# Pooled attention and two MLPs on one core: flat keys and values, longer query reads, low words on VectorE

## The chip, the cores and the metric

One core of a Trainium2 chip runs the kernel. The metric is device time in microseconds, from the first to the last instruction of one launch with a little around it; lower is better. The engines are TensorE (PE: matrix products into PSUM), VectorE (DVE: elementwise work and reductions), ScalarE (ACT: elementwise functions with a scale and a bias), GpSimd (POOL: elementwise work in SBUF) and SyncE (SP: it issues DMA). GpSimd also issues some DMAs. Each engine runs its instructions in order; semaphores order them between engines.

## The reference

```python
# q, k, v: (8, 8, 576, 64); pool = 8, Sp = 576 / 8 = 72
k_p = k.reshape(B, H, Sp, pool, D).mean(axis=3)
v_p = v.reshape(B, H, Sp, pool, D).mean(axis=3)
scores = np.matmul(q, k_p.transpose(0, 1, 3, 2)) / np.sqrt(D)
attn = softmax(scores)                          # exp, sum + 1e-9, divide
x = np.matmul(attn, v_p)                        # -> (B*S, H*D) = (4608, 512)
h = x @ moe_w_in                                # (512, 2048)
x = np.where(h >= 1, h, np.where(h <= -1, 0, (h + 1) ** 2 / 4)) @ moe_w_out
h = x @ moe2_w_in
return (h * sigmoid(h)) @ moe2_w_out            # (4608, 512)
```

So there are 8 batches of 576 queries, each with 72 pooled keys and values per head, and two MLPs over all 4608 rows. The weights arrive as 64-bit floats, and the kernel reads them as pairs of 32-bit words.

## The kernel before

**Number form.** Each MLP product is made from two half-precision words, high and low: `three` adds high x high, high x low and low x high in one PSUM accumulation. Every weight is converted on the chip. For each piece of a weight the chain is: `look` (VectorE, the largest magnitude), a scale found from it by `w_scale` (six tiny VectorE instructions on as many columns as there are pieces in the group), `signed` (ScalarE, line 208), `shifted` and `with_low` (VectorE, lines 109 and 216), a scaling pass on ScalarE (283 or 240), a cast to the high word on ScalarE (285 or 245), and the low word as a subtraction (286 or 246). The constants LO1 and LO2 say which pieces of the first MLP's two weights have that subtraction on VectorE: pieces 3 and 7 of the first weight, piece 0 of the second. GpSimd makes the others. The first weight has nine pieces (seven of 256 columns and two of 128), the second eight.

**Attention.** Query rows go in 36 tiles of 128. Tiles 0 to 3 make up token tile 0, the 512 rows of the first product. For tiles 0 to 8 (batches 0 and 1) attention runs in 32-bit floats: `att_qT` transposes the queries on TensorE, `att_scores` multiplies with the pooled keys in block form (`k32`), finds the largest score per head and subtracts it on VectorE, and exponentiates on ScalarE; `att_norm` sums, takes the reciprocal on VectorE and multiplies on GpSimd; `att_T` transposes the weights head by head (eight transposes); `att_pv` multiplies with the pooled values (16 matmuls) and `split` writes the high and low words of x. Later tiles use half-precision words and DMA transposes.

Keys and values are pooled by sums. In batch 0 the keys come head by head, 72 partitions of 2 KB each, and are reduced on VectorE, two heads on GpSimd; the values come in two halves of four heads and are summed by GpSimd (`halving`). From batch 1 on half of each group of eight rows is loaded, the other half is added by an accumulating DMA that GpSimd issues (`kv_more`), and VectorE adds the rest (lines 468 and 471).

**Order.** The code is emitted in the order wanted, and the framework places instructions on the engines by its own estimate of time. `tick` releases the parts of the conversion at steps that lists name: LOOK_AT, SCALE_AT, C1_AT (the nine pieces of the first weight), B1_AT (keys and values of batch 1), W2_AT and MORE2_AT (the second weight), SLOTS_AT (attention of tiles 4 to 7). Steps below zero lie in the attention of tiles 0 to 3, steps 1 to 18 in the first product of token tile 0 (`emit_h`, one step per 128 columns of 2048; `pre_A`, `min_A`, `mid_A`, `post_A`, `split_g` then apply the activation), later steps in its second product (`yA`). Each released part is held behind the last product, activation and VectorE instruction before it (`behind`). SyncE issues the loads in order: keys of batch 0, queries, values, the nine pieces, the later queries, batch 1, the second weight. The first weight's last four pieces are loaded into the room of the second weight's tiles w2[0] to w2[3].

After token tile 0 the kernel runs the remaining eight token tiles of the first MLP and then the second MLP with TensorE full.

Of the kernel before, what the change touches and what calls it, by code (L numbers as in the profile page):

```python
# [11 lines left out]
I32 = mybir.dt.int32  # L12
# [22 lines left out]
def tile_pooled_attention_two_mlps(  # L35
# [99 lines left out]
    cols, free, free2 = const.tile([128, 136], F32, name="cols"), iter(range(46)), iter(range(45))  # L135
    spread = cols[:, 46:136].rearrange("p (n u) -> p n u", u=2)
# [4 lines left out]

    def apart(n):
        i = [next(free2) for _ in range(n)][0]
        return spread[:, i:i + n, 0]
# [47 lines left out]
    def w_scale(e, d, s, g, up=14):  # L192


        t = sm.tile([128, 8, 2], F32, tag="wt", name="wt", bufs=2)[:, :, 0]
        a, b = (t[:, 4 * i:4 * i + g.shape[1]] for i in range(2))
        ts(a, g, FLOOR_HIGH, DOWN, ALU.max, ALU.mult)
        ts(b.bitcast(I32), a.bitcast(I32), EXP_MASK, op0=ALU.bitwise_and)
        bits(d, b, -1.0, 15 + TOP)
        ts(b.bitcast(I32), a.bitcast(I32), 0x00700000, 3, ALU.bitwise_and, ALU.logical_shift_left)  # L200
        bits(s, b, -1.0, 254 - 8 * TOP + up)
        ts(e.bitcast(I32), a.bitcast(I32), 0x7FF00000, 3, ALU.bitwise_and, ALU.logical_shift_left)
# [11 lines left out]
    def with_low(x, r):  # L214
        xi = x.bitcast(I32)
        return nc.vector.scalar_tensor_tensor(  # L216
            out=xi, in0=low(r), scalar=29, in1=xi, op0=ALU.logical_shift_right, op1=ALU.bitwise_or
        )

    def steps(piece, dst, scale, loaded, fill=None):  # L220
# [17 lines left out]
        def s3():  # L238
            x = t["x"]
            nc.scalar.activation(out=x, in_=x, func=AF.Copy, scale=scale()[1])  # L240
            if fill:
                fill(x)
                return
            hi, lo, eng = dst()
            nc.scalar.copy(out=hi, in_=x)  # L245
            eng.tensor_tensor(out=lo, in0=x, in1=hi, op=ALU.subtract)  # L246
# [7 lines left out]
    def weight_in(w, e, tiles, cuts, rooms):  # L254
# [4 lines left out]
        mx, s, g, down = (apart(n) for _ in range(4))  # L259
# [16 lines left out]
        def work(p):  # L276
# [6 lines left out]
            nc.scalar.activation(out=x, in_=x, func=AF.Copy, scale=s[:, p:p + 1])  # L283
            hi, lo = tiles[p][:, 0], tiles[p][:, 1]
            nc.scalar.copy(out=hi, in_=x)  # L285
            (nc.vector if p in LO1 else nc.gpsimd).tensor_tensor(out=lo, in0=x, in1=hi, op=ALU.subtract)  # L286
# [99 lines left out]

    SPT = (SP + 15) // 16 * 16
    NE = 2 * S // 128
    v16 = [bp.tile([SP, 2, H, D], F16, name=f"v16{j}") for j in range(2)]
    v32 = [x.rearrange("p a h d -> p (a h d)").bitcast(F32).rearrange("p (h d) -> p h d", h=H) for x in v16]  # L390
    both16 = bp.tile([128, 2, 2, 4, 128], F16, name="e16")
    e16 = [both16[:, j] for j in range(2)]
    km, vm = col(), col()
# [23 lines left out]

    def kv_load(b, which):
        if (b, which) == (0, "k"):
            for h in range(H):  # L420
                r = gp.tile([128, 2, N], F16, tag="g", name="k0").rearrange("p a n -> p (a n)").bitcast(F32)
                r = kv_raw[b, which, h] = r[0:SP].rearrange("p (r d) -> p r d", r=POOL)
                nc.sync.dma_start(out=r, in_=k[0, h].rearrange("(p r) d -> p r d", r=POOL))
            return
        if b == 0:
            src = v[0].rearrange("h (p r) d -> p h r d", r=POOL)
            for j in range(2):
                r = kv_raw[b, which, j] = kvp.tile([SP, 4, POOL, D], F32, tag="raw", name="v0", bufs=2)
                for a, b_ in PARTS:
                    nc.sync.dma_start(out=r[a:b_], in_=src[a:b_, 4 * j:4 * j + 4])  # L430
            return
# [3 lines left out]

    def kv_more(b, which):
        for a, b_ in PARTS:
            nc.gpsimd.dma_start(
                out=kv_raw[b, which][a:b_], in_=kv_rows(b, which)[a:b_, :, HALF:POOL], accum_op=ALU.add
            )  # L440

    def halving(to, r):

        plus(r[:, 0:4], r[:, 0:4], r[:, 4:8])
        plus(r[:, 0:2], r[:, 0:2], r[:, 2:4])
        plus(to, r[:, 0], r[:, 1])

    def kv_pool(b, which, j):
        if j == 0 and which == "v" and b < 2:
            sums[b, which] = v32[b]  # L450
        elif j == 0:
# [3 lines left out]
        if (b, which) == (0, "k"):  # L455
            for h in (2 * j, 2 * j + 1):
                r, to = kv_raw.pop((b, which, h)), sums[b, which][0:SP, h]
                if h in K_POOL:
                    halving(to, r)
                else:  # L460
                    nc.vector.tensor_reduce(out=to, in_=r.rearrange("p r d -> p d r"), axis=AX.X, op=ALU.add)
        elif b == 0:
            if j < 2:
                r = kv_raw.pop((b, which, j)).rearrange("p h r d -> p r h d")
                halving(sums[b, which][0:SP, 4 * j:4 * j + 4], r)
        elif j == 2:
# [25 lines left out]
    def keys32(b):  # L492
        ps = att_ps([128, NP, 128])
        x = sums.pop((b, "k"))
        for p in range(NP):
            nc.tensor.transpose(
                out=ps[:, p, 0:SP], in_=x[0:SP, 2 * p:2 * p + 2].rearrange("p h d -> p (h d)"),
                identity=ident[0:SP, 0:SP],
            )
        for h in range(2):  # L500
            r = slice(64 * h, 64 * h + 64)
            nc.scalar.copy(out=k32[b][r, :, h], in_=ps[r, :, 0:SP])
# [16 lines left out]
    def values_mean(b):  # L519
        junk = v16[b % 2] if b > 1 else ap.tile([SPT, H, 2, D], F16, tag="krows", name="by", bufs=2)[0:SP]  # L520
        sums_mean(sums[b, "v"][0:SP], vm, junk)

    def values_scale(b):
        if b not in vscale:
            vscale[b] = search(SP, vm, ev[:, b:b + 1])
# [17 lines left out]
    def load_q(i):  # L543
        if i == NI - 1:
            q_t[i] = up.tile([128, N], F32, tag="u", name="q3").rearrange("p (h d) -> p h d", h=H)
        else:
            q_t[i] = qp.tile([128, H, D], F32, tag="q", name="qt")
# [3 lines left out]
    def att_qT(i):  # L551

        qt = q_t.pop(i)
# [21 lines left out]
    def att_scores(i):  # L575
# [19 lines left out]
        if i in (2, 5):  # L595
            e = both16.rearrange("p f a h n -> p (f a h n)").bitcast(F32)[:, 0:H * SP]
            e = e.rearrange("p (h s) -> p h s", h=H)
# [23 lines left out]
    def att_norm(i):  # L621
# [7 lines left out]
        nc.gpsimd.tensor_tensor(  # L629
            out=e, in0=e, in1=den.unsqueeze(2).to_broadcast([128, H, SP]), op=ALU.mult  # L630
        )
        for hf, x in enumerate(e16 if i >= NE else ()):
# [4 lines left out]
    def att_T(i):  # L637
        e = at_t.pop(i)
        for hf in range(2):
            if i < NE:  # L640
                ps = att_ps([SP, 4, 128])
                for h in range(4):
                    nc.tensor.transpose(out=ps[:, h], in_=e[:, 4 * hf + h], identity=ident)
                aT_t[i, hf] = ap.tile([SP, 4, 128], F32, tag="aT", name="aT32", bufs=3)
# [700 lines left out]
```

## Time and profile before

| | |
|---|---|
| median of 3 runs | 1581.48 us (1579.86 to 1581.96) |
| the profiled execution's own time | 1581.64 us |
| its span, first to last instruction | 1579.8 us |
| busy: PE, DVE, ACT, POOL | 1530.5, 1172.5, 894.4, 568.9 us |
| granted TensorE clock, mean | 0.981 |

The profile is one execution of the kernel on the chip. A page of it gives the busy time of every engine and 40 slices of the span, in which a digit is the busy share in tenths. From the trace behind it come views: groups of instructions by source line and shape, the waits of an engine with what released it, stretches of time with the busy time of every engine, the instructions in order of time, the DMA traffic, and the chain of work that ended last. An instruction of a helper such as `ts` carries the helper's line, so one is told apart by the tile it writes (`wa` and `wb` are the first and second weight's words, `xf` a piece in conversion, `hps` the first product).

### The profile page before, as it was taken

To read this page: it belongs to the slowest core of one execution; us is meant where nothing else is said; L and a number is where in the kernel's file an instruction comes from. 1 tells how busy PE (TensorE), PEld (TensorE's weight loads), DVE (VectorE), ACT (ScalarE), POOL (GpSimd) and SP (SyncE) were. 2 spreads that over 40 slices of the span, in tenths; PEclk is the share of its full clock that TensorE was granted. 3 is DMA by queue.
4 is the path that set the end of the run, shared out by engine and by line. 5 is a ranking of instruction groups with operands and counts; after the bars stand their busy time and mean duration, and the time that the engine had idled before them with its cause. 6 is when DMAs were issued, how large, how long until landed. Compare 5 with 4: busy or idle time off the path is not lost.

```text
span 1579.8 us, 34130 instructions
## 1 busy us (share of the span) xinstructions
PE 1530.5 (97%) x14210; PEld 1060.0 (67%) x14210; DVE 1172.5 (74%) x2120; ACT 894.4 (57%) x1397; POOL 568.9 (36%) x507
## 2 busy tenths in 40 slices
PE   7769899999999999999999999999999999999998
PEld 5335454444444444444444599999999999999997
DVE  7999588777877778767657577777777777777765
ACT  3776666576756667645665554554454445454443
POOL 5423223134423344312556034433333444333322
PEclk7889999999999999999999999999999999999999
DMA  9963669859468594538662420001000000000000
GB/s 278 191 135 102 136 151 179 159 130 179 88 144 120 121 160 102 115 91 243 237 241 87 154 97 28 29 28 42 28 29 28 29 28 29 28 28 29 29 15 28
DMA packets 207627, 161.73 MB, mean 102 GB/s; under 512 B 136432, under 2 KB 175088, under 8 KB 207472
## 3 DMA queue, kind: packets, MB, share of 16 engines
q1 hardware_dynamic: 198064, 151.29, 36.9%
q0 software_dynamic: 9408, 8.27, 4.1%
q8 instruction: 111, 1.82, 0.5%
q14 instruction: 44, 0.36, 0.1%
HBM read 102.76 MB, written 33.55 MB: 86 GB/s over the span
## 4 chain that ended last, share of the span: by engine, by line
PE 82%; DVE 7%; DMA 4%; ACT 4%; issue 2%; POOL 1%; SPq 1%; DVEq 0%; ACTq 0%; POOLq 0%
PE hb L149 7%; PE hb L147 7%; PE hb L148 7%; PE y L1051 7%; PE y L1053 7%; PE y L1052 7%; PE y L147 6%; PE y L149 6%; PE y L148 6%; PE hps L148 6%; PE hps L147 6%; PE hps L149 6%; PE att L685 1%; DVE xf L216 1%; DVE g L861 1%
## 5 line engine op out<-in xcount | busy, mean ns | idle before, releaser
L147 PE MATMUL hb<-xh,wc 128*128 128x128 f16 x2016 | 347.6, 219 | 0.0
L148 PE MATMUL hb<-xl,wc 128*128 128x128 f16 x2016 | 347.6, 219 | 0.0
L149 PE MATMUL hb<-xh,wc 128*128 128x128 f16 x2016 | 347.6, 219 | 0.0
L372 DVE SCALAR_TENSOR_TENSOR g<-c,small,g 128x512 f16<-128x512 f32 x252 | 228.7, 910 | 82.1 <-ACT g L371 82.1
L1052 PE MATMUL y<-wd,g 128*128 128x256 f16 x1008 | 274.7, 273 | 0.0
L1053 PE MATMUL y<-wd,g 128*128 128x256 f16 x1008 | 274.7, 273 | 0.0
L1051 PE MATMUL y<-wd,g 128*128 128x256 f16 x1008 | 274.7, 273 | 0.0
L991 ACT ACTIVATE c<-c,small 128x512 f32<-128x512 f32 x144 | 103.2, 717 | 228.1 <-DVE c L988 228.1
L147 PE MATMUL hps<-xh,wa 128*128 128x512 f16 x576 | 221.4, 385 | 9.3 <-ACT wa L285 8.1
L371 ACT ACTIVATE g<-c,small 128x512 f16<-128x512 f32 x252 | 177.6, 718 | 85.7 <-POOL c L121 48.2
L149 PE MATMUL hps<-xh,wa 128*128 128x512 f16 x576 | 220.1, 383 | 4.7 <-POOL wa L286 2.7
L148 PE MATMUL hps<-xl,wa 128*128 128x512 f16 x576 | 221.4, 384 | 0.2 <-DVE xl L372 0.2
L149 PE MATMUL y<-g,wb 128*128 128x512 f16 x544 | 207.6, 382 | 4.0 <-POOL wb L246 2.9
L988 DVE TENSOR_TENSOR c<-c,hb 128x512 f32<-128x512 f32 x252 | 168.7, 681 | 55.1 <-PE hb L149 52.9
L148 PE MATMUL y<-g,wb 128*128 128x512 f16 x544 | 208.0, 382 | 1.0 <-DVE g L890 1.0
L147 PE MATMUL y<-g,wb 128*128 128x512 f16 x544 | 208.1, 383 | 0.3 <-ACT wb L245 0.3
L148 PEld LDWEIGHTS <-wc 128*128 128x128 f16 x2016 | 197.3, 98 | 2.4
L147 PEld LDWEIGHTS <-wc 128*128 128x128 f16 x2016 | 197.3, 98 | 2.2
L149 PEld LDWEIGHTS <-wc 128*128 128x128 f16 x2016 | 197.3, 98 | 0.0
L861 DVE SCALAR_TENSOR_TENSOR g<-g,small,u 128x512 f32<-128x512 f32 x144 | 125.5, 873 | 61.5 <-ACT u L857 59.7
L118 POOL TENSOR_TENSOR c<-c 128x512 f32<-128x512 f32 x108 | 164.1, 1534 | 2.8
L850 ACT ACTIVATE g<-hps,small 128x512 f32<-128x512 f32 x144 | 111.2, 773 | 80.8 <-PE hps L149 74.2
(178 smaller groups left out, 2621.9 us busy)
## 6 DMA issues: line engine op xcount, KB each, us to landing
raw<-in_moe_w_out_dram SPq DMA_DIRECT2D x21, 1024.0 KB
raw<-in_moe_w_in_dram SPq DMA_DIRECT2D x18, 1024.0 KB
y<-y SPq DMA_DIRECT2D x36, 256.0 KB
yin<-y SPq DMA_DIRECT2D x18, 512.0 KB
out_dram<-ob SPq DMA_DIRECT2D x36, 256.0 KB
d<-hl SPq DMA_DIRECT2D x32, 256.0 KB
qt<-in_q_dram SPq DMA_DIRECT2D x31, 256.0 KB
wc<-d SPq DMA_DIRECT2D x8, 896.0 KB
```

The costliest lines, as they stand in the source:

```text
L118: nc.gpsimd.tensor_tensor(out=out, in0=a, in1=b, op=ALU.subtract)
L147: nc.tensor.matmul(out=acc, lhsT=wh, rhs=xh, start=start, stop=False)
L148: nc.tensor.matmul(out=acc, lhsT=wh, rhs=xl, start=False, stop=False)
L149: anchor["pe"] = nc.tensor.matmul(out=acc, lhsT=wl, rhs=xh, start=False, stop=stop)
L371: a = nc.scalar.activation(out=hi, in_=x, func=AF.Copy, scale=s)
L372: return a, nc.vector.scalar_tensor_tensor(out=lo, in0=x, scalar=s, in1=hi, op0=ALU.mult, op1=ALU.subtract)
L850: nc.scalar.activation(out=w, in_=h_t.pop(s), func=AF.Relu, scale=c_A(r, "c1", s), bias=r["br"])
L861: anchor["dve"] = nc.vector.scalar_tensor_tensor(out=g32_t[s], in0=g32_t[s], scalar=r["br"], in1=u_t.pop(s), op0=ALU.subtract, op1=ALU.max)
L988: nc.vector.tensor_tensor(out=out, in0=x, in1=y, op=ALU.add)
L1051: nc.tensor.matmul(out=acc, lhsT=xh, rhs=wh, start=start, stop=False)
L1052: nc.tensor.matmul(out=acc, lhsT=xh, rhs=wl, start=False, stop=False)
L1053: nc.tensor.matmul(out=acc, lhsT=xl, rhs=wh, start=False, stop=stop)
```

## The change

- Keys and values of batches 0 and 1 are laid out flat: the 576 groups of (head, pooled row) fill 128 partitions four times and 64 once, a group's eight rows being one run of 2 KB (1 KB for the halves in batch 1). `keys32` brings them back to heads by matmuls with slices of the identity. For the values, `att_T` transposes the softmax weights flat, in five transposes, and `att_pv` multiplies with `vpair`, a pair of heads masked out of a flat block by eight ScalarE copies, and with the rest of the next block.
- Tile 0's queries are read in runs of 1 KB (four rows of one head per partition) by two DMAs into the room of w2[3]; a copy per tile (VectorE for tiles 0 to 2, ScalarE for 3) brings 128 of them together. Row order in token tile 0 changes, and the output write undoes it. The first weight's last piece, whose room that was, is loaded after the last of these copies.
- The low words of all nine pieces of the first weight, and of pieces 0, 1, 2 and 6 of the second, are made on VectorE by `split`: one scaled ScalarE copy and one VectorE instruction on two SBUF inputs. The separate scaling pass goes there.
- `w_scale` works on one column at a time; the spaced columns (`apart`) go.
- Attention weights of tiles 0, 1 and 3 are normalised on VectorE.
- The steps of some pieces move (C1_AT, MORE2_AT, W2_AT), `c1` is computed on ScalarE.

```diff
-    K_POOL = (3, 6)
+    K_POOL = (2, 3)
+    NORM_V = (0, 1, 3)
+    Q_V = (0, 1, 2)
+    V0_V = ()
-    C1_AT = [-6, -3, -2, 2, 2, 3, 4, 10, 12]
+    C1_AT = [-6, -3, -2, 2, 5, 3, 5, 8, 12]
-    MORE2_AT = 13
+    MORE2_AT = 12
-    W2_AT = [[7, 10, 12, 13, 17, 18], [19, 19, 19, 19, 19, 19], [21, 21, 21, 21, 23, 23], [27, 27, 27, 27, 27, 27]]
+    W2_AT = [[7, 10, 12, 13, 17, 18], [19, 19, 19, 19, 19, 19], [21, 21, 21, 21, 23, 23], [27, 27, 27, 27, 29, 29]]
-    LO1 = (3, 7)
-    LO2 = (0,)
+    LO1 = (0, 1, 2, 3, 4, 5, 6, 7, 8)
+    LO2 = (0, 1, 2, 6)
...
     def w_scale(e, d, s, g, up=14):
-        t = sm.tile([128, 8, 2], F32, tag="wt", name="wt", bufs=2)[:, :, 0]
-        a, b = (t[:, 4 * i:4 * i + g.shape[1]] for i in range(2))
-        ts(a, g, FLOOR_HIGH, DOWN, ALU.max, ALU.mult)
...
+        n = range(g.shape[1])
+        a, b, c = ([t[:, 3 * i + j:3 * i + j + 1] for i in n] for j in range(3))
+        for i in n:
+            ts(a[i], g[i], FLOOR_HIGH, DOWN, ALU.max, ALU.mult)
...
+    def halve(x, s, hi, lo, by_vector):
+        if by_vector:
+            split(hi, lo, x, s)
+            return
+        nc.scalar.activation(out=x, in_=x, func=AF.Copy, scale=s)
+        nc.scalar.copy(out=hi, in_=x)
+        minus(lo, x, hi)
...
-            nc.scalar.activation(out=x, in_=x, func=AF.Copy, scale=s[:, p:p + 1])
-            hi, lo = tiles[p][:, 0], tiles[p][:, 1]
-            nc.scalar.copy(out=hi, in_=x)
-            (nc.vector if p in LO1 else nc.gpsimd).tensor_tensor(out=lo, in0=x, in1=hi, op=ALU.subtract)
+            halve(x, s[:, p:p + 1], tiles[p][:, 0], tiles[p][:, 1], p in LO1)
...
+    def kv_groups(b, which):
+        return (k if which == "k" else v)[b].rearrange("h (p r) d -> (h p) (r d)", r=POOL)
+    def grouped(out, src, a, b, cols, dma):
+        w = slice(*cols)
+        if b > a and a < FULL:
+            e = min(b, FULL)
+            x = src[128 * a:128 * e, w].rearrange("(c p) x -> p c x", p=128)
+            dma(out=out[:, 0:e - a], in_=x)
+        if b > FULL:
+            dma(out=out[0:LASTC, FULL - a], in_=src[128 * FULL:, w])
...
+            else:
+                r = kv_raw.pop((b, which))
+                halving(x[:, 0:FULL], r[:, 0:FULL], vplus)
+                halving(x[0:LASTC, FULL:NC], r[0:LASTC, FULL:NC], vplus)
...
     def load_q(i):
+        if i < NI:
+            if i == 0:
+                q_t["all"] = w2[KD - 1].rearrange("p a c f -> p (a c f)").bitcast(F32).rearrange(
+                    "p (h j d) -> p h j d", h=H, j=NI
+                )
+                for h in range(0, H, 4):
+                    nc.sync.dma_start(
+                        out=q_t["all"][:, h:h + 4].rearrange("p h j d -> p h (j d)"),
+                        in_=q[0, h:h + 4, 0:N].rearrange("h (p j) d -> p h (j d)", j=NI),
+                    )
+            return
...
+        w = (nc.vector if i in NORM_V else nc.gpsimd).tensor_tensor(
             out=e, in0=e, in1=den.unsqueeze(2).to_broadcast([128, H, SP]), op=ALU.mult
         )
...
+                nc.tensor.matmul(
+                    out=ps[:, c, s], lhsT=vpair[b][:, h:h + 2].rearrange("p a d -> p (a d)"),
+                    rhs=aT_t[i, 0][:, c, s], start=True, stop=False,
+                )
+                m = (h + 2) * SP - 128 * (c + 1)
+                nc.tensor.matmul(
+                    out=ps[64:128, c, s], lhsT=sums[b, "v"][0:m, c + 1],
+                    rhs=aT_t[i, 0][0:m, c + 1, s] if c + 1 < FULL else aT_t[i, 1][:, s], start=False, stop=True,
+                )
+                nc.tensor.matmul(
+                    out=ps[0:64, c, o:o + 1], lhsT=k32[b][0:16, 0, 1, 0:64], rhs=aT_t[i, 0][0:16, c, o:o + 1],
+                    start=False, stop=True,
+                )
...
-    q_to(3)
+    q_to(4)
     kv_load(0, "v")
-    q_to(4)
-    for p in range(len(cuts1)):
+    for p in range(len(cuts1) - 1):
         load1(p)
...
+        if n == NI - 1:
+            load1(len(cuts1) - 1)
```

## Rows read from the trace of the kernel before

**Rows 1.** The page: busy tenths of TensorE in 40 equal slices of the span.
```profile
PE   7769899999999999999999999999999999999998
```

**Rows 2.** Stretches: start and end, length, busy time (instructions) of each engine, clock, DMA.
```profile
core 0: us, PE busy (x) PEld busy (x) DVE busy (x) ACT busy (x) POOL busy (x), PEclk, DMA share, GB/s
14.00:48.50 34.50, 24.81 (x154) 19.03 (x154) 30.58 (x73) 19.04 (x27) 15.22 (x12) 0.70 1.08 303
48.50:113.60 65.10, 52.38 (x224) 22.88 (x222) 59.93 (x99) 49.66 (x71) 24.63 (x14) 0.87 0.75 157
113.60:125.70 12.10, 5.51 (x23) 3.83 (x22) 11.99 (x18) 10.14 (x14) 1.82 (x2) 0.72 0.42 114
```

**Rows 3.** Waits of TensorE, 20 to 190 us: in total, times, longest.
```profile
PE hps L147 <- ACT wa L285: 8.1, 2, 7.4
...
PE hps L149 <- POOL wa L286: 2.7, 2, 2.4
...
PE y L149 <- DVE wb L246: 1.0, 1, 1.0
```

**Rows 4.** VectorE in order of time, 13 to 110 us: start, duration, instruction [idle before].
```profile
13.97 0.46 DVE L604 TENSOR_REDUCE mx<-early 128x4 f32<-128x288 f32 x1 [3.26 <-PE early L589]
...
20.45 1.96 DVE L625 TENSOR_SCALAR den<-den 128x8 f32<-128x8 f32 x1
...
49.61 2.12 DVE L111 TENSOR_SCALAR wt<-wt 128x3 int32<-128x3 int32 x1
...
52.78 3.98 DVE L111 TENSOR_SCALAR small<-cols,small 128x9 f32<-128x9 f32 x1
...
66.34 1.22 DVE L468 TENSOR_TENSOR raw<-raw 72x1024 f32<-72x1024 f32 x1 [0.99 <-DMA raw<-in_k_dram]
...
72.80 2.06 DVE L216 SCALAR_TENSOR_TENSOR xf<-wb,xf 128x1024 int32<-128x1024 int32 x1
...
76.05 6.45 DVE L468 TENSOR_TENSOR raw<-raw 72x1024 f32<-72x1024 f32 x1
...
108.12 1.40 DVE L109 TENSOR_SCALAR u<-g,small 128x512 f32<-128x512 f32 x1
```

**Rows 5.** VectorE grouped by line and form, 0 to 190 us: count, busy, mean ns, idle.
```profile
L109 DVE TENSOR_SCALAR u<-g,small 128x512 f32<-128x512 f32 x17 | 8.9, 532 | 2.2 <-ACT g L850 2.1
L216 DVE SCALAR_TENSOR_TENSOR xf<-raw,xf 128x1024 int32<-128x1024 int32 x7 | 8.5, 1216 | 0.0
...
L111 DVE TENSOR_SCALAR cols<-wt 128x3 int32<-128x3 int32 x6 | 0.9, 163 | 0.1
```

**Rows 6.** GpSimd in order of time, 48 to 110 us.
```profile
48.45 3.26 POOL L286 TENSOR_TENSOR wa<-xf,wa 128x1024 f16<-128x1024 f32 x1 [8.65 <-ACT wa L285]
52.30 2.27 POOL L438 DMA_DIRECT2D raw<-in_k_dram  x2 [0.60 <-POOL wa L286]
53.80 2.93 POOL L286 TENSOR_TENSOR wa<-xf,wa 128x1024 f16<-128x1024 f32 x1
...
69.30 4.47 POOL L286 TENSOR_TENSOR wa<-xf,wa 128x512 f16<-128x512 f32 x1 [10.54 <-ACT wa L285]
...
76.44 4.96 POOL L286 TENSOR_TENSOR wa<-xf,wa 128x1024 f16<-128x1024 f32 x2
...
107.11 2.13 POOL L286 TENSOR_TENSOR wa<-xf,wa 128x1024 f16<-128x1024 f32 x1 [14.63 <-ACT wa L285]
```

**Rows 7.** DMA packets of two stretches, 0 to 20.5 us and 20.5 to 43 us.
```profile
DMA packets 5634, 3.77 MB, mean 184 GB/s; under 512 B 4304, under 2 KB 4304, under 8 KB 5634
...
DMA packets 5366, 8.23 MB, mean 366 GB/s; under 512 B 945, under 2 KB 1969, under 8 KB 5364
```

**Rows 8.** ScalarE grouped by line and form, 0 to 190 us.
```profile
L283 ACT ACTIVATE xf<-xf,cols 128x1024 f32<-128x1024 f32 x7 | 8.0, 1149 | 4.9 <-DVE xf L216 4.8
```

**Rows 9.** SyncE in order of time; then the chain of waits at 53 us.
```profile
44.77 1.68 SPq L434 DMA_DIRECT2D raw<-in_k_dram  x2
...
53.18 13.06 DMA raw<-in_k_dram
```

**Rows 10.** The chain of waits, in order of time, at 180 us.
```profile
180.49 0.87 PE att L643 x8
```

More of the change, by code (lines that the diff above doesn't have):

```diff
@@ L258, in weight_in @@
         held, n = {}, len(cuts)
-        mx, s, g, down = (apart(n) for _ in range(4))
+        mx, s, g, down = (col(n) for _ in range(4))
         def load(p):
@@ L442, in halving, with group_sums @@
[L442 to L446, printed above, removed]
-    def kv_pool(b, which, j):
-        if j == 0 and which == "v" and b < 2:
-            sums[b, which] = v32[b]
-        elif j == 0:
+            accumulate(kv_raw[b, which][a:b_], kv_rows(b, which)[a:b_, :, HALF:POOL])
+    def group_sums(b, which):
+        if (b, which) == (1, "v"):
+            x = both32[:, H * SP:H * SP + NC * D].rearrange("p (c d) -> p c d", d=D)
+        else:
+            x = kvp.tile([128, NC, D], F32, tag="sum", name="gsum", bufs=2)
+        sums[b, which] = x
+        nc.gpsimd.memset(x[LASTC:128, FULL], 0.0)
+        return x
@@ L454, in kv_pool @@
                 nc.gpsimd.memset(sums[b, which][SP // 32 * 32:SPT], 0.0)
[L455 to L466, printed above, removed]
+        if j == 2:
             r = kv_raw[b, which]
@@ L492, in keys32 @@
     def keys32(b):
-        ps = att_ps([128, NP, 128])
         x = sums.pop((b, "k"))
[L495 to L502, printed above, removed]
+        ps = att_ps([128, NP, SP])
+        for h in range(H):
+            for c in range(h * SP // 128, ((h + 1) * SP - 1) // 128 + 1):
+                a, e = max(h * SP, 128 * c), min((h + 1) * SP, 128 * c + 128)
+                n = 128 if c < FULL else LASTC
+                nc.tensor.matmul(
+                    out=ps[h % 2 * 64:h % 2 * 64 + 64, h // 2, a - h * SP:e - h * SP], lhsT=x[0:n, c],
+                    rhs=ident[0:n, a - 128 * c:e - 128 * c], start=True, stop=True,
+                )
+        nc.scalar.copy(out=k32[b][0:64, :, 0], in_=ps[0:64])
+        (nc.vector.tensor_copy if b == 0 else nc.scalar.copy)(out=k32[b][64:128, :, 1], in_=ps[64:128])
     krows = {}
@@ L519, in values_mean @@
     def values_mean(b):
-        junk = v16[b % 2] if b > 1 else ap.tile([SPT, H, 2, D], F16, tag="krows", name="by", bufs=2)[0:SP]
-        sums_mean(sums[b, "v"][0:SP], vm, junk)
+        if b > 1:
+            sums_mean(sums[b, "v"][0:SP], vm, v16[b % 2])
+            return
+        x = sums[b, "v"]
+        junk = ap.tile([128, NC * D], F32, tag="krows", name="by", bufs=2)
+        nc.scalar.activation(
+            out=junk, in_=x.rearrange("p c d -> p (c d)"), func=AF.Abs, scale=1.0 / (H * D), accum_out=vg,
+        )
+        for h in range(H):
+            nc.scalar.activation(out=vpair[b][:, h], in_=x[:, h // 2], func=AF.Copy, scale=mine[:, h:h + 1])
     def values_scale(b):
         if b not in vscale:
-            vscale[b] = search(SP, vm, ev[:, b:b + 1])
+            vscale[b] = search(SP, vm if b > 1 else vg, ev[:, b:b + 1])
     def batch_values(b):
@@ L551, in att_qT @@
     def att_qT(i):
-        qt = q_t.pop(i)
+        if i < NI:
+            qt = qp.tile([128, H, D], F32, tag="q", name="qt")
+            (nc.vector.tensor_copy if i in Q_V else nc.scalar.copy)(out=qt, in_=q_t["all"][:, :, i])
+        else:
+            qt = q_t.pop(i)
         if i < NE:
@@ L703, in tile_pooled_attention_two_mlps @@
     CW = DFF // PIECES
-    w2 = [w2p.tile([128, 2, KF, 128], F16, name=f"wb{d}") for d in range(KD)]
     cuts3 = [(p * CW, (p + 1) * CW) for p in range(PIECES)]
@@ L1084, in slot @@
                 att_qT(n)
-            if r == 3 and first <= n - 2:
+            if r == (0 if n - 2 == NE - 1 else 3) and first <= n - 2:
                 att_pv(n - 2)
+                if n - 2 == NE - 1:
+                    nc.gpsimd.memset(both16[:, :, :, :, SP:], 0.0)
             if r and first <= n - 1 < end:
```

185 lines of the change are left out of this document (123 added, 62 removed).

## The prediction

> **What bounds the kernel now.** I read the slices of the span first. TensorE is at nine tenths from about 190 us to the end; all that is lost lies in the first eighth [rows 1]. The diff touches later code only in one small constant per token tile and in the address of four output writes, so whatever it is worth has to be read from this first stage: it is worth what it moves the point from which TensorE runs without gaps.
>
> The table by stretches splits the stage at its own marks [rows 2]. From 14 to 48.5 us attention of the first four query tiles runs, and tile 0's first product goes on only after it. From 48.5 to 113.6 us that product runs: TensorE has 52.38 us of work in 65.1, VectorE is busy in 59.93, ScalarE in 49.66. From 113.6 to 125.7 us TensorE has 5.51 us of work and VectorE 11.99 of 12.1. So VectorE sets the pace up to 125.7 us. TensorE's waits agree: 8.1 us for a weight piece from ScalarE, 2.7 for a low word from GpSimd [rows 3]; both are ends of the conversion of a piece, which passes VectorE twice.
>
> Then I looked at what fills VectorE. Some instructions are far too long: three columns 2.12 us (usually 0.163), nine columns 3.98 (I leave 0.3, an estimate from the three), 1024 words 2.06 (usually 1.216), a sum of 1024 words 6.45 (else 1.22), 512 words 1.40 (usually 0.53) [rows 4, 5]. The worst lie beside GpSimd's low words and end with them: 49.61 + 2.12 = 51.73 against 48.45 + 3.26 = 51.71; 52.78 + 3.98 = 56.76 against 53.80 + 2.93 = 56.73; the sum ends 1.1 us, its own length, after 76.44 + 4.96 = 81.40 [rows 4, 6]. These are stalls behind GpSimd. Over the usual lengths: 2.0 + 3.7 + 0.8 + 5.2 + 0.9 = 12.6 of the 59.93 us.
>
> **The change part by part.** Durations are from one profiled execution of 1581.64 us (span 1579.8, so 1.84 us around it); the median of the runs shown is 1581.48.
>
> *Loads.* Keys and values of batches 0 and 1 go from 72 to 128 partitions, the queries of tile 0 from 256 B to 1 KB runs. Up to 20.5 us the DMA moved 184 GB/s on average, with 4304 of 5634 packets under 512 B; after it 366 GB/s [rows 7]. The 3.4 MB of keys, values and queries take 18.5 us at the first rate and 9.3 at the second; with something lost at the start they could land some 7 us sooner, and the first weight behind them (its last piece is now issued later, since the queries sit in its room, but it is also looked at last). That is not worth 7 us: the first score maximum starts at 13.97 us [rows 4], and from there VectorE is busy 30.58 of 34.5 us [rows 2]. What it has to do before 48.5 us is 30.58 less one stall (1.96 where 0.16 is usual [rows 4]) = 28.8, and the change adds three norms (576 words, somewhat over half of the 1.216 for 1024) at 0.7, three copies of 512 words at 0.53, piece 0's low word at 1.25, 18 more instructions on single columns (0.07 each, under the 0.163 of three columns since they overlap) and half a key copy, 0.4: 2.1 + 1.6 + 1.25 + 1.3 + 0.4 = 6.65, so 35.5 us [rows 5]. Tile 0 needs both query loads; from about 13 us it ends at 48.5 if VectorE hardly waits, which earlier tiles and pieces allow. I take 0; ends -3 (it starts at 10.5 us) and +5 (it waits as now). Eight small ScalarE copies follow the sums of the values, and nothing waits behind them at that time.
>
> *Low words of the first weight, and the scales, 48.5 to 113.6 us.* Six of GpSimd's low words lie here, five of 1024 and one of 512 words [rows 6]. On VectorE I take 1.25 (two inputs of 1024 words are 1.216) and 0.75: 5 x 1.25 + 0.75 = 7.0 us more [rows 5]. Scales add 12 x 0.07 = 0.8; batch 1's sums, 960 words for 1536 each, give back 1.2. The stalls go, 12.6. VectorE: 59.93 - 12.6 + 7.0 + 0.8 - 1.2 = 53.9 us. Its idle time is 5.2 of 65.1 now; ScalarE, for which part of it waits, loses one pass of 1.149 us (less for half pieces) per piece, some 7 us, and gains about 2 in value copies [rows 8]. So I take 3 us idle: 56.9 for 65.1, -8.2 us. Ends: -12 (no idle; piece 7 is released two steps sooner and the wait for ScalarE goes) and +4 (hardly a stall goes).
>
> What could be late next is VectorE's sum of batch 1's keys: it already waits 0.99 us for an accumulating load of 13.06 us, which is on the chain; the first half of these keys was issued by SyncE only at 44.77 us [rows 4, 9], and GpSimd's part of the load stood behind the low word that ended at 51.71 [rows 6]. Now the keys' buffer is free from the start and no low word stands ahead, so I let it land about 8 us sooner and cost nothing. Everything of the stage is queued behind that sum on VectorE.
>
> *Second weight, 113.6 to 186 us.* Of its low words the second, third and seventh move to VectorE, where the first is already; ScalarE's extra pass goes for the four. The product waits 1.0 us for the first low word [rows 3], and the dense run starts then, at 125.7. I take -1.5 (ends -4 and +2: VectorE is full just there). GpSimd keeps the fourth to sixth and the eighth, and what TensorE waits for them.
>
> *TensorE in tiles 4 to 8.* Five transposes for eight of 0.87 us: 0.33 less per tile [rows 10]. The products with the values become eight larger and four tiny matmuls for sixteen small ones; I take no change. 5 x 0.33 = 1.6, of which I count 1.0 as on the path. The late edits (a constant on ScalarE, four strided writes, a moved fill on GpSimd) lie beside saturated TensorE: 0; without that cover under 1 us each.
>
> Sum: 0 - 8.2 - 1.5 - 1.0 = -10.7; 1581.64 - 10.7 = 1570.9, and 1571 beside the median.
>
> A rule that speaks against the change: the Trainium skill, "SBUF — State Buffer", Who interferes with whom, says that a VectorE instruction with two SBUF inputs and a GpSimd instruction that reads SBUF shut each other out for a whole instruction. The sum held for 5.2 us agrees [rows 4]. By it the new low words and norms are exposed wherever GpSimd still reads SBUF; that is the mechanism of the third rival, whose price is worked out from rows.
>
> **The rivals.** One: the stalls go, but VectorE then waits for the accumulated keys. For: it waited 0.99 us already and now gets there sooner by the first two stalls, 5.7 us. Against: the earlier issue. If the load lands when it does now, 0.99 + 5.7 = 6.7 us are handed back: 1571 + 6.7 = 1578.
>
> Two, more is won: the loads let VectorE start at 10.5 us, ScalarE's relief takes its idle time, and the first low word comes at once: -3 - 12 - 3 - 1 = -19, 1563. For: in the main stretch TensorE lost 12.7 us to gaps and ran at a granted 0.87, which is time at the lower of its two levels, 1.2 GHz. Against: VectorE at 0.92 already.
>
> Three, slower: VectorE is the bound, and loading it is what counts. The attention stretch has 35.5 us of work at the present share of busy time (30.58 of 34.5) from the present start: 5 us later. In the next stretch the stalls stay and change their cause (the new two-input instructions are held by norms, value sums and load issues on GpSimd): 7.0 + 0.8 - 1.2 = +6.6. With -4 from the second weight and -1 from TensorE that is +6.6, 1588. It decides from the point where less than half of the 12.6 us goes and the first product starts later than 49 us. For: the fullest engine gets the work, and the held instruction of 52.78 us began beside a load issue on GpSimd. Against: the stalls end with low words that are gone.
>
> **How the numbers follow.** Forecast 1571, chance 0.5, with its own range 1565 to 1577; one 0.18 at 1578; two 0.18 at 1563; three 0.14 at 1588. A change within 0.2% (1578.3 to 1584.6) can't be told from none. Faster: 0.49 of the forecast, 0.18 of rival two and 0.08 of rival one, whose 1578 lies on the bound: 0.75. Same: the rest of these, 0.11. Slower: rival three, 0.14. For 8 in 10 I go from 1560, which leaves out the best part of rival two, to 1585, which leaves out most of rival three.
>
> **What would show it.** In the profile after: no low word of the first weight on GpSimd, and no VectorE row over 2 us while the first product runs; about 54 us of VectorE in about 57 there; the first product going on at 46 to 50 us; the accumulated keys landing before VectorE asks for them; the small packets gone from the first 15 us; the dense run of the second weight from about 115 instead of 125.7 us; and TensorE saturated from then on as before, so that the gain at that point is the gain at the end. It is wrong if VectorE's long rows reappear beside other GpSimd work, if the first product starts after 52 us, or if the end moves by another amount than the dense run's start.

## The result: slower by 0.6 per cent

The changed kernel takes 1590.62 us (median of 4 runs, 1588.91 to 1591.93) where the kernel before, run on the same chip, takes 1580.78. The ratio is 1.0061, with a 95% interval of 1.0044 to 1.0079. The forecast was 1571 us, in a range of 1560 to 1585: the sign is wrong, and the time lies above the range. The profiled execution of the changed kernel took 1589.66 us, with a span of 1587.8.

Where the two profiled executions part is read from a few marks: the first product's matmuls going on without a break, the second product's first matmul, and SyncE's writing of a token tile's result (that of token tile 0, of 2 and of 7; the nine token tiles are numbered from 0).

| mark, us | before | after | without the new value products (e1) |
|---|---|---|---|
| first product goes on | 48.55 | 54.88 | 50.07 |
| second product, first matmul | 122.24 | 118.55 | 112.94 |
| token tile 0 written | 184.49 | 183.31 | 172.65 |
| token tile 2 written | 377.63 | 382.71 | 367.43 |
| token tile 7 written | 822.47 | 829.32 | 813.28 |
| span | 1579.8 | 1587.8 | 1571.7 |

So the first product starts 6.3 us late, is 10.0 us shorter (63.7 for 73.7), and what follows it up to the first result is 2.5 us longer: 1.2 us are won there. Token tiles 1 and 2 give back 6.3 us, tiles 3 to 7 another 1.8, the rest 1.1. The marks and spans come from one profiled execution of each kernel. That of the kernel before took 1581.64 us, more than its median, and those of the changed kernel and of e1 took less than theirs, so that spans differ by some microseconds from what the ratios of medians give.

### The profile page after: what moved, and what is told of

Same layout as the page of the kernel before. It is cut to its first block, busy times and chain, and to the rows that moved or that the text cites. A ratio compares the mean times of both kernels' runs of the same rounds, so it can differ in the third digit from the quotient of the medians.

```text
span 1587.8 us, 34349 instructions
## 1 busy us (share of the span) xinstructions
PE 1556.5 (98%) x14303; PEld 1077.7 (68%) x14303; DVE 1160.0 (73%) x2167; ACT 885.9 (56%) x1409; POOL 538.9 (34%) x499
## 4 chain that ended last, share of the span: by engine, by line
PE 55%; DVE 12%; issue 11%; POOL 8%; ACT 8%; DMA 6%; SPq 0%; DVEq 0%; POOLq 0%; ACTq 0%
PE y L145 7%; PE y L147 6%; PE y L146 6%; PE hps L146 6%; POOL c L121 6%; PE hps L147 6%; PE hps L145 6%; DMA yin<-y 4%; DVE g L381 2%; PE y L1163 2%; PE y L1164 2%; PE y L1165 2%; POOL c L124 2%; PE hb L147 2%; PE hb L146 2%
```

## The profile after

First the slices of the page, TensorE's busy tenths and granted clock, against [rows 1].

```profile
PE   7979999999999999999999999999999999999998
PEclk7789999999999999999999999999999999999999
```

TensorE is busier at the start than before and at the lower of its levels for longer. The same three stretches as in [rows 2], with the same columns:

```profile
14.00:48.50 34.50, 29.86 (x138) 21.63 (x136) 25.27 (x67) 13.28 (x29) 7.70 (x11) 0.59 1.10 332
48.50:113.60 65.10, 57.05 (x271) 26.92 (x268) 62.37 (x152) 51.78 (x79) 9.44 (x8) 0.88 0.61 123
113.60:125.70 12.10, 9.95 (x39) 5.63 (x40) 10.90 (x16) 6.87 (x10) 0.54 (x1) 0.72 0.48 144
```

In the first, TensorE has 29.86 us of work where it had 24.81, and VectorE 25.27 where it had 30.58 and was expected to have more. The engines have changed places. Shorter stretches show how far:

```profile
22.00:30.00 8.00, 7.99 (x33) 5.78 (x34) 8.00 (x29) 2.01 (x4) 1.16 (x1) 0.50 1.06 373
30.00:40.00 10.00, 10.00 (x44) 7.16 (x44) 3.98 (x5) 4.15 (x7) 2.35 (x2) 0.50 1.13 313
40.00:50.00 10.00, 10.00 (x44) 6.55 (x42) 6.79 (x20) 2.42 (x4) 1.14 (x2) 0.50 1.08 255
50.00:56.00 6.00, 6.00 (x23) 3.96 (x22) 5.13 (x24) 3.82 (x4) 1.06 (x2) 0.50 0.93 166
```

From 22 to 56 us TensorE is never idle and its granted clock is 0.50, 1.2 GHz. From 30 to 40 us VectorE is idle for 6 of 10 us and waits for TensorE, as its rows in order of time show (start, duration, instruction, idle before it and what ended it):

```profile
40.30 0.43 DVE L285 TENSOR_REDUCE cols<-all 128x2 f32<-128x256 f32 x1 [5.14 <-PE all L282]
...
113.04 1.38 DVE L112 TENSOR_SCALAR u<-g,small 128x512 f32<-128x512 f32 x1
```

The second row is VectorE's longest between 14 and 125 us: the stalls of [rows 4] are gone. GpSimd's rows show why, against [rows 6]: no low word is left between 48 and 111 us.

```profile
48.86 2.20 POOL L478 DMA_DIRECT2D raw<-in_v_dram  x2 [9.52 <-DMA raw<-in_v_dram]
75.44 2.27 POOL L478 DMA_DIRECT2D raw<-in_k_dram  x2 [24.38 <-DVE u L112]
...
111.21 2.93 POOL L723 TENSOR_TENSOR e<-e,den 128x576 f32<-128x576 f32 x1 [22.89 <-DVE den L722]
```

What fills TensorE are the products with the values. Here are its rows for one query tile, four pairs of heads, at the lower level (L780 is the full-width matmul, L785 the part in the next block, L789 the tiny closing one; an f32 matmul is two rows, an f32 transpose one):

```profile
25.39 0.76 PE L780 MATMUL att<-aT,v 128*128 128x128 f32 x2
26.08 0.47 PE L785 MATMUL att<-aT,gsum 16*64 16x128 f32 x1
26.09 0.37 PE L789 MATMUL att<-aT,k 16*64 16x1 f32 x2
26.35 0.42 PE L785 MATMUL att<-aT,gsum 16*64 16x128 f32 x1
26.70 0.80 PE L780 MATMUL att<-aT,v 128*128 128x128 f32 x2
...
28.04 0.80 PE L780 MATMUL att<-aT,v 128*128 128x128 f32 x2
28.76 0.69 PE L785 MATMUL att<-aT,gsum 48*64 48x128 f32 x2
29.38 0.36 PE L789 MATMUL att<-aT,k 16*64 16x1 f32 x2
29.68 0.80 PE L780 MATMUL att<-aT,v 128*128 128x128 f32 x2
...
31.02 0.36 PE L789 MATMUL att<-aT,k 16*64 16x1 f32 x2
31.32 0.42 PE L743 MATMUL early<-ident,e 128*64 128x128 f32 x1
```

The tile's product lasts from 25.39 to 31.32: 5.9 us. The tiny matmul starts with the partial one where that has 16 rows (26.08 and 26.09), and after it where it has 48 (28.76, then 29.38). Before, sixteen rows of two times 64 columns did it in 1.98 us at this level and in 1.03 at the full clock:

```profile
32.75 1.98 PE L685 MATMUL att<-aT,v 72*64 72x128 f32 x16
...
217.73 1.09 PE L685 MATMUL att<-aT,v 72*64 72x128 f32 x16
218.76 0.43 PE L583 MATMUL att<-kT,qT 128*128 128x72 f16 x8
```

(These three are of the kernel before, beyond the rows shown ahead of the prediction.) Later in the changed kernel, at the full clock, a tile's product stands among the products of a token tile:

```profile
214.43 0.38 PE L147 MATMUL hps<-xh,wa 128*128 128x512 f16 x1
214.65 0.38 PE L780 MATMUL att<-aT,v 128*128 128x128 f32 x2
214.96 0.32 PE L785 MATMUL att<-aT,e 16*64 16x128 f32 x1
...
217.85 0.27 PE L789 MATMUL att<-aT,k 16*64 16x1 f32 x2
218.05 0.66 PE L678 MATMUL att<-kT,qT 128*128 128x72 f16 x8
218.52 0.62 PE L145 MATMUL hps<-xh,wa 128*128 128x512 f16 x1
218.93 0.63 PE L146 MATMUL hps<-xl,wa 128*128 128x512 f16 x1
```

It takes 3.40 us (214.65 to 218.05) instead of 1.03, and the large matmuls behind it come every 0.41 us instead of every 0.22: the clock fell to its lower level. Query tile 4, which holds tokens of two batches and so has eight blocks, takes 5.66 us (126.78 to 132.44), and the eight large matmuls behind it (from 132.67) come every 0.42 or 0.43.

## Experiments

Theory A: the products with the values are what went wrong, in the first stage and after it. Theory B: VectorE became the bound through the low words. Theories C and D put a loss on the late edits. Ratios are to the kernel before on the same chip, with 95% intervals. The edits are shown in short: words and angle brackets stand for code that is left out.

**e1, the old form of the values.** Loads, sums, transposes and products of the values as before, all else as changed.

```
-    <grouped sums of v, vpair, 5 transposes, the matmuls of L780, L785 and L789>
+    <loads and sums of v by head, 8 transposes>
+    for c in range(2):
+        nc.tensor.matmul(out=ps[64 * c:64 * c + 64, h // 2, o:o + n],
+                         lhsT=sums[b, "v"][0:SP, h + c], rhs=a[:, (h + c) % 4, o:o + n])
```

> The changed kernel with the values of batches 0 and 1 put back into the form of before: loaded and summed on 72 partitions, eight transposes of the attention per tile, sixteen 64-column matmuls per tile for the products with the values. Keys, queries, low words and scales stay as changed. Theory A (the product with the values is what went wrong: 3.40 us of TensorE per tile at the full clock where before had 1.03, 5.9 at the lower level where before had 1.98): tiles 4 to 8 lie on saturated TensorE and give back 5 x 2.4 = 12 us less 1.6 for the transposes; in tiles 0 to 3 the first product starts some 6 us sooner than its 54.9 us. Time 1568 to 1576, faster than before. Theory B (the low words on VectorE and the late first product are the loss): the values matter little and the time stays at 1585 or more. Theory C (the late edits, the output rows and the constant on ScalarE, cost it in the saturated part): 1585 or more as well, and tile 1 to tile 8 still take 6 us longer than before.

Measured: 1575.64 us, ratio 0.9973 (0.9962 to 0.9984). Theory A holds, and B and C fall: with the same low words and late edits the kernel is faster than before. The table above has its marks. Of the 16.1 us of span between it and the changed kernel, 4.8 lie ahead of the first product, 0.8 in it, 5.1 between the second product and the first result, 4.6 in token tiles 1 and 2 and 0.8 later. By the two ratios the values cost 0.88 per cent, 14 us. e1 puts back the loads, sums and transposes of the values together with their products; e7 and e8 price the products by themselves.

**e2, two halves.** The full-width matmul as two of 64 columns, without the tiny one.

```
-  matmul(out=ps[:, c, s], lhsT=<pair, 128 columns>)   # and the tiny closing matmul
+  for a in range(2):
+      matmul(out=ps[64 * a:64 * a + 64, c, s], lhsT=vpair[b][:, h + a], start=True, stop=a == 0)
```

> The changed kernel with one edit: the 128-column matmul of a pair of heads is two 64-column ones on the two halves of the columns, each with its own start, so that the tiny closing matmul goes too. Theory A1 (what costs is the form: the full-width matmul and the tiny one each run alone, where two 64-column ones run beside each other): a tile's product falls from 3.40 us to 2.0 to 2.6 at the full clock, 5 x 1 us in tiles 4 to 8 and about as much in the first stage: 1578 to 1584. Theory A2 (only the number of columns counts, and the halves stream as many): 3.0 us or more per tile and 1588 to 1591. Theory B (the product is not the cause): 1590, no change.

Measured: 1594.61 us, ratio 1.0097 (1.0083 to 1.0111). Neither came: it is slower still. The product did get cheaper, here at the lower level:

```profile
27.18 0.70 PE L781 MATMUL att<-aT,v 128*64 128x128 f32 x4
27.80 0.69 PE L786 MATMUL att<-aT,gsum 16*64 16x128 f32 x2
28.42 0.70 PE L781 MATMUL att<-aT,v 128*64 128x128 f32 x4
...
32.14 0.42 PE L743 MATMUL early<-ident,e 128*64 128x128 f32 x1
```

Four rows of two halves take 0.62 us (27.18 to 27.80), and the two rows of the next block's part, with nothing beside them, take 0.62 as well. A tile needs 4.96 us instead of 5.93 there, and 2.91 instead of 3.40 at the full clock, between the two forecasts; the first product starts 1.3 us sooner (53.61). But token tile 0 is written at 189.03, 5.7 us later than in the changed kernel. The order of the steps on VectorE and ScalarE, which a planner makes from its own costs, came out another way: between 56 and 125 us ScalarE waits 7.7 us for VectorE's u where it waited 0.6.

The two lines are of e2, then of the changed kernel (in total, times, longest):

```profile
ACT u L966 <- DVE u L112: 7.7, 3, 2.9
```

```profile
ACT u L969 <- DVE u L112: 0.6, 1, 0.6
```

So e2 does not tell A1 from A2 by its time. That the order alone makes the 5.7 us is an inference; no run here held the order fixed.

**e3, the tiny matmul twice.**

```
+  for last in (False, True):
       matmul(out=ps[0:64, c, o:o + 1], lhsT=<16 rows of zeros>, start=False, stop=last)
```

> The changed kernel with the tiny closing matmul (16 rows, one column, adds zeros) issued twice each. It prices the tiny ones, which can't simply be left out. Theory A (they run alone for most of their 0.2 us because of their weight load): 4 to 5 more per tile, 0.8 to 1.2 us at the full clock and 1.2 to 1.6 at the lower, so 5 us in tiles 4 to 8 and up to 5 in the first stage: 1596 to 1600. Rival (they hide beside their neighbours): 1590 to 1592.

Measured: 1597.82 us, ratio 1.0116 (1.0100 to 1.0132). The time lies in the range of theory A, but that is luck. The span grows by 8.0 us for 40 more matmuls, and 0.2 us is what a tiny one with nothing beside it takes in the rows above (217.85 to 218.05); the second one of a pair adds less, as e3's rows of the second and the fourth block of a tile show, at the lower level:

```profile
42.42 0.80 PE L780 MATMUL att<-aT,v 128*128 128x128 f32 x2
...
43.76 0.80 PE L780 MATMUL att<-aT,v 128*128 128x128 f32 x2
...
45.61 0.80 PE L780 MATMUL att<-aT,v 128*128 128x128 f32 x2
...
46.96 0.58 PE L790 MATMUL att<-aT,k 16*64 16x1 f32 x4
47.47 1.65 PE L282 MATMUL all<-ident,cols 128*128 128x128 f32 x6
```

The block from 42.42 to 43.76, whose partial matmul has 32 rows, takes 1.34 us, as in the changed kernel (26.70 to 28.04): the added one hides. That from 45.61 to 47.47, with 64 rows, takes 1.86 for 1.64. So a tile grows by some 0.4 us at the lower level and by 0.23 at the full clock (3.64 for 3.41), about 2.5 us in the eight tiles other than tile 4. Tile 4's product takes 7.93 us for 5.66, its second half at a granted clock of 0.50; the rest of the 8.0 us is not accounted for by these rows.

**e4, the conversions alone.** The kernel before with the low words on VectorE, the scales column by column and the new places of these steps.

```
-    LO1 = (3, 7)
-    LO2 = (0,)
+    LO1 = (0, 1, 2, 3, 4, 5, 6, 7, 8)
+    LO2 = (0, 1, 2, 6)
```

> The kernel before with only the conversion part of the change: low words of the first weight and of four halves of the second on VectorE, scales column by column, the constant on ScalarE and the new places of these steps. Attention, loads and outputs as before. By the prediction's terms (-8.2 in the first product, -1.5 in the second weight): 1571 to 1573. Theory A lets this stand and expects 1570 to 1577. Theory B (VectorE is the bound, its new work costs): 1584 or more, with stalls of VectorE behind other GpSimd work in the stretch from 48 to 113 us.

Measured: 1575.69 us, ratio 0.9982 (0.9972 to 0.9991), which is 2.8 us (1.4 to 4.4) of a forecast of 9.7; the spans of the two profiled executions differ by 7.1. The direction of this part of the sum stands, its size at the end does not. Rival one shows up in it: with the old loads, VectorE waits 2.2 us for the accumulated keys.

**e5 and e6, queries and output rows.** e5 is e1 with token tile 0's queries and the four output writes as before; e6 is e4 with those two as changed.

```
-  q_t["all"] ... in_=q[0, h:h + 4, 0:N].rearrange("h (p j) d -> p h (j d)", j=NI)
-  to = out[0:N, :].rearrange("(p j) f -> p j f", j=NI)[:, r0 // 128]
+  q_t[i] = qp.tile([128, H, D], F32, ...)
+  to = out[r0:r0 + 128, :]
```

> The version with the old values (e1), and with the queries of token tile 0 and the four output writes too as before: of the change stay the flat keys, the low words on VectorE and the scales. The stage of the last two matmuls took 643.4 us in the changed kernel and 643.5 in e1, against 641.1 before and 641.4 in e4, which has plain output rows. Theory D (the four output writes in strided rows cost 2.2 us there): that stage falls to 641.3 and the time from 1575.6 to about 1573. Rival (the 1 KB query loads are what makes e1's start): the first stage gets 3 to 5 us longer and the time is 1576 to 1580.

> The kernel before with the conversion part (e4) and with the queries of token tile 0 in 1 KB runs, hence the four output writes in strided rows. Theory D: the last stage rises from 641.4 to 643.5 us, and as the first stage waits for VectorE and not for loads, the time is 1576 to 1579 against 1575.7 for e4. Rival (the rows cost nothing, the queries bring the start forward): the last stage stays at 641 and the time falls to 1570 to 1574.

Measured: e5 1573.32 us, ratio 0.9960 (0.9947 to 0.9972), the lowest median of all, though its interval overlaps those of e1 and e11; e6 1579.66, ratio 0.9996 (0.9988 to 1.0005). The times came out much as theory D had them (e6's 0.7 above its range), but theory D is wrong: the last stage, from the first read-back of y that follows token tile 8 to the end, took 640.8 us in e6, with strided rows, and 642.4 in e5, with plain ones. What e6 lost lies in the first stage: token tile 0 is written at 183.06 us, against 178.64 in e4. With the flat keys the same queries cost nothing there: 172.65 us in e1, 173.92 in e5. In the last stage the slower kernels have tiles in which the read-back of y lands late. VectorE's rows for it in e5:

```profile
1082.83 1.22 DVE L136 TENSOR_REDUCE m<-yin 128x1 f32<-128x1024 f32 x1 [3.21 <-DMA yin<-y]
1119.85 1.22 DVE L136 TENSOR_REDUCE m<-yin 128x1 f32<-128x1024 f32 x1 [1.86 <-DMA yin<-y]
```

Issued at 1077.84 and 1116.20, they landed after 4.99 and 3.65 us. The stage takes 640.8 to 641.3 us in the five kernels without flat keys (before, e4, e6, e9, e10) and 642.4 to 644.5 in the eight with them; why is open, and with it 2.4 of the 8.0 us of span that the change costs.

**e7 and e8, the price of a product.** The changed kernel with the products of query tiles 0 to 3 (e7), or 5 to 8 (e8), computed twice.

```
-            for o, n, b, _ in segs(i):
+            for o, n, b, _ in segs(i) * (2 if i < NI else 1):     # e8: i > NI
```

> The changed kernel with the products with the values of query tiles 0 to 3 computed twice each (the second time over the first). It prices them in the first stage: 4 x 5.9 us at the lower clock level. Theory A (between 22 and 54 us TensorE has become the bound through them): the first product starts some 20 us later than 54.9 and the time is 1606 to 1614. Rival B (VectorE sets the pace there, TensorE's work lies beside it): 1591 to 1597.

> The changed kernel with the products with the values of query tiles 5 to 8 computed twice each. They lie beside the first product, in the second weight's stretch and in token tile 1. Theory A (3.4 us each on saturated TensorE, and a stretch at the lower clock level behind some): 4 x 3.4 = 14 us at most and 7 at least, as tiles 5 to 7 may fall where TensorE waits for weights: 1598 to 1605. Rival (the first stage alone carries the loss): 1591 to 1594.

Measured: e7 1621.53 us, ratio 1.0261 (1.0248 to 1.0275). The first product starts at 79.76, 24.9 us later, 6.2 for each of the four tiles: nothing hides them, TensorE is the bound there. The time lies above both forecasts, since a further 7.8 us are lost between the second product and the first result (72.5 for 64.8), which no product was added to; why is open. e8 1615.33 us, ratio 1.0221 (1.0204 to 1.0239): 25 us more, not 7 to 14. The product is dearer than its 3.4 us, because the clock falls inside a doubled one:

```profile
202.09 0.32 PE L785 MATMUL att<-aT,e 32*64 32x128 f32 x1
202.10 0.27 PE L789 MATMUL att<-aT,k 16*64 16x1 f32 x2
202.25 0.27 PE L785 MATMUL att<-aT,e 32*64 32x128 f32 x1
...
206.20 0.80 PE L780 MATMUL att<-aT,v 128*128 128x128 f32 x2
206.92 0.69 PE L785 MATMUL att<-aT,e 64*64 64x128 f32 x2
...
212.07 0.63 PE L147 MATMUL hps<-xh,wa 128*128 128x512 f16 x1
```

It began at 200.12 at the full clock; from about 203.6 on its rows have the lengths of the lower level, it lasts 9.4 us instead of 6.8, and the large matmuls behind it still come at 0.43 up to 213.8. The four doubled products take 7.5, 8.9, 9.4 and 7.3 us, where single ones take 3.4 or 3.5.

**e9 and e10, the two conversions apart.** e9 is e4 with the wide scales of before; e10 is the kernel before with the scales alone.

```
e9:   LO1, LO2 and the places of e4, w_scale and the constant of before
e10:  w_scale and the constant of e4, LO1, LO2 and the places of before
```

> The kernel before with the low words alone: those of the first weight and of four halves of the second go to VectorE, with the new places of these steps; the scales stay several columns wide, as before. The prediction's sum for the first product (stalls -12.6, low words +7.0, scales +0.8) says that the stalls go with the low words on GpSimd, so this alone gives what e4 gave (1575.7), at most 1 us less or more: 1574 to 1577. Rival (the wide scales stall behind other GpSimd work as well, and only single columns avoid it): 1579 or more, with rows of 2 us and over on VectorE for 3 or 9 columns.

> The kernel before with the scales alone: column by column, the nine products of the constant on ScalarE; low words as before on GpSimd. By the prediction's sum the instruction that follows the wide one is held by the same low word of GpSimd, so the stalls stay and 0.8 us come on top: 1580 to 1583. Rival (single columns are not held, or ScalarE's constant takes the stall of 3.98 us away): 1574 to 1578.

Measured: e9 1581.18 us, ratio 1.0009 (1.0000 to 1.0018); e10 1580.58, ratio 1.0002 (0.9994 to 1.0011). e10 is as forecast. e9 is not: alone the low words bring nothing. The rival's time came without its rows: the wide scales do not stall, and the only VectorE row over 2 us in its first product is a two-input step of the conversion, 2.18 us for 1.21, from 111.47, beside a norm on GpSimd (111.17 to 112.56). Its second product starts at 118.67, 3.6 us sooner than before, but what it wins it loses behind that point, token tile 0 being written at 183.90. TensorE's row of the stretch from 150 to 160 us in e9, and then in e4, shows one of the places:

```profile
150.00:160.00 10.00, 6.21 (x22) 2.53 (x24) 9.60 (x19) 8.11 (x8) 5.10 (x3) 0.70 0.84 145
```

```profile
150.00:160.00 10.00, 10.00 (x60) 5.06 (x58) 7.63 (x17) 1.11 (x2) 2.58 (x2) 1.00 0.41 114
```

In e9 TensorE waits there for a low word of the second weight from GpSimd (2.2 us) and for steps of ScalarE and VectorE (1.0 and 0.7), and its clock falls; in e4 it is full. VectorE's wait for the accumulated keys is 4.1 us in e9, against 2.2. Whether the scales prevent this by their own time or by the order that the planner then finds is not settled.

**e11, the norms back on GpSimd.** e5 with `NORM_V = ()`.

> The best version so far (e5: flat keys, low words on VectorE, scales by column, old values, queries and outputs) with the norms of query tiles 0, 1 and 3 back on GpSimd. They were counted at 0.7 us each of VectorE's work ahead of the first product, and GpSimd needs about 3 us for one. If VectorE sets the pace there, the first product starts some 2 us sooner and the time is 1571 to 1573; if the tile waits for its slowest norm, it starts 1 to 5 us later: 1574 to 1578.

Measured: 1575.28 us, ratio 0.9970 (0.9958 to 0.9982). The intervals of e5 and e11 overlap: the norms on VectorE are worth nothing that these runs can tell. GpSimd needs 1.15 us for one in tiles 0 to 3 of e11, not the 3 that was expected.

## Why the prediction was wrong, step by step

- **The step that failed** is "The products with the values become eight larger and four tiny matmuls for sixteen small ones; I take no change". It was a term without a row and without bounds, and its count mixes units: by the code it is twelve matmuls for eight, which the profile shows as 24 rows for sixteen (the "16 matmuls" of the kernel's description are rows). Measured: 3.40 us for 1.03 in a query tile at the full clock, 5.66 for 1.09 in tile 4, 5.9 for 1.98 at the lower level, and stretches of large matmuls at 1.2 GHz behind three of them. In tiles 4 to 8 that is 4.6 + 4 x 2.4 = 14 us of TensorE, against the 1.6 that the transposes save. e1 shows the loss of the values in all: 16.1 us of span, 5.6 of them ahead of the second product and 10.5 behind its start.
- **Loads and attention, 0 (-3 to +5): +6.3.** The small packets went (193 of 3717 under 512 B in the first 20.5 us, against [rows 7]) and VectorE had its data in time (from 10 to 50 us it waits 1.9 us for a load), but the bound of this stretch became TensorE, which no rival named. Without the new form of the values the step is +1.5 (e1), within its ends.
- **First product, -8.2, and first low word of the second weight, -1.5: -10.0** from the first matmul of the one to the first of the other. The mechanism is the one forecast: the stalls of [rows 4] are gone, batch 1's key sums start without a wait at 67.05 us, and VectorE's low words take 1.28 us, 1.25 expected. Between these two marks VectorE has 60.36 us of work in 63.67, where before it had 68.41 in 73.69: 8.1 us less, where 6.0 were forecast for the stretch to 113.6. That neither part of the conversion brings anything alone (e9, e10) was not foreseen.
- **TensorE saturated from then on as before, so that the gain at that point is the gain at the end: no.** The second product started 3.7 us sooner and the end came 8 us later. TensorE was not saturated there before; these lines are of before, then of the changed kernel:

```profile
125.70:186.00 60.30, 55.76 (x326) 29.34 (x327) 42.36 (x89) 31.00 (x40) 24.07 (x15) 0.94 0.51 117
```

```profile
125.70:186.00 60.30, 59.96 (x335) 33.82 (x333) 37.61 (x86) 27.04 (x37) 16.49 (x11) 0.97 0.47 114
```

  Before, TensorE had 4.5 us of gaps there; the changed kernel has 0.3, no room beside which the products could hide. Without the new values (e1) token tile 0 is written 11.8 us sooner than before and the span is 8.1 us shorter, and by its ratio the kernel gains 0.27 per cent, 4.3 us, against the 10.7 of the sum: the rest of the change was overrated too. In e9 the second product starts 3.6 us sooner, and nothing is left at the end.
- **Late edits, 0:** the output rows cost nothing in the last stage (e6). The 2.4 us lost there go with the flat keys, by a way that no run showed.
- **The rivals.** Rival three had the sign and nearly the time (1588), but not the cause: VectorE was not the bound, and the stalls did not come back (over the first product and the second weight's start it has 6.6 less 4, measured are -10.0), so that its nearness is luck. The stall behind a norm that it named does occur, once, in e4 and e9: 2.18 us for 1.21. Rival one was real, though not here: VectorE waits 2.2 and 4.1 us for the accumulated keys in e4 and e9, which keep the old loads; in the changed kernel the sums start without a wait, as argued from the earlier issue. Two of the prediction's own signs of being wrong came: the first product starts after 52 us, and the end moved otherwise than the second product's start.

The rows of before held a warning. TensorE's groups from 18 to 190 us give a row of the old product 304 ns on average, and yet sixteen fit into 1.03 us: two of 64 columns run beside each other. [Rows 10] gives eight single 128-column passes 0.87 us, 0.11 each. The new product has 24 rows, of which those of full width have nothing beside them, and the partial ones only the tiny one, in two blocks of four.

The Trainium skill, "TensorEngine Tiling (Array Packing)", Key Properties, says that parts of the array work independently, and that a change of the partition into parts drains the engine; its Instruction Overhead says that a matmul of one column takes as long as one of some sixty. The trace agrees with the first as far as it goes: two 64-column matmuls take 0.62 us together and the partial one takes 0.62 alone (e2). A one-column f32 matmul with nothing beside it takes 0.20 us (217.85 to 218.05), but no run has one of sixty columns to compare. How much of a block's 0.67 to 0.98 us is a drain no run here shows.

## What to carry to other kernels

When a change gives a matmul another shape, price it by the rows of its own group in order of time, from start to start, and not by its count or its sum of busy time, and count both forms in the same unit: matmuls that used half of the array each were running two at a time, and a fuller-looking form can take three times as long. A term set at "no change" needs two ends like any other. A gain at the point from which an engine is saturated reaches the end only if nothing is added to that engine behind the point, and if the steps planned behind it stay where they were.

## What the runs showed of the hardware

- The granted clock stood at 0.50 (1.2 GHz) from 22 to 56 us while TensorE was busy without a break with f32 matmuls and transposes. It rose within the large f16 matmuls of the first product, and fell inside the doubled f32 products of e8.
- A 64-column f32 matmul of 16 rows and one of a single column next to it overlap (26.08 and 26.09), and so does one of 32 rows (202.09 and 202.10 in e8); those of 48 and 64 rows do not (28.76, then 29.38; 30.40, then 31.02).
- Two f32 matmuls of 64 columns on the two halves take together what one alone takes (0.62 us at 1.2 GHz).
- A VectorE step with two inputs that starts beside a norm on GpSimd takes 2.18 us instead of 1.21 and ends 1.1 us after the norm (e9, 111.47 against 111.17 to 112.56).
